# PSUM places in a fixed turn, an earlier emptying of the P V bank, and a respaced preparation table

## The chip, the cores and the metric

The kernel runs on one core of one Trainium2 chip. The metric is the device time of one execution in microseconds; the time of a kernel is the median of its runs. Five engines of the core matter here: TensorE (PE in the profile; PEld is its loading of the stationary operand), VectorE (DVE), ScalarE (ACT), GpSimd (POOL) and SyncE (SP), which issues most of the transfers.

## The reference

The computation is an attention whose queries are pooled by two, and a mixture of experts behind it that sends every row to one expert. Cut to what matters:

```python
# attention: q, k, v are (8 batches, 8 heads, 1152, 64); pooled queries: 576 per head
q_pool = q.reshape(B, H, S // 2, 2, D).mean(axis=3)
scores = (1 / sqrt(D)) * q_pool @ k^T
scores = scores - max(scores, axis=-1)
attn   = exp(scores); attn = attn / (sum(attn) + 1e-9)
x      = attn @ v                      # heads side by side: x is (4608, 512)
# experts: 8 of them, w1 (512, 1024), w2 (1024, 512)
logits = x @ w_gate
e_idx  = argmax(logits);  gate_w = softmax(logits)[e_idx]
eom    = sigmoid(x @ w_output_gate)
for e in range(8):
    m = e_idx == e
    out[m] = gate_w[m] * eom[m, e] * (relu(x[m] @ w1[e]) @ w2[e])
```

All inputs and the output are float32. The kernel splits operands into a high and a low part and adds the products, so that low-precision passes of TensorE give the accuracy of float32.

## The kernel before, in words

**Stages.** The attention takes the first two thirds of the time, the experts the rest. The attention runs over 32 pairs, a pair being two heads of one batch, four pairs to a batch. A pair takes 18 steps, one for each block of 128 keys of each head; below, "step 13" is the step with number 13 of its pair, counted from 0. The instructions of TensorE, VectorE, ScalarE and GpSimd run in the order in which the program writes them; the main loop over `s` (step) is that order.

**A step** writes, in this order: the low-part subtraction of the step before, where VectorE has it (`lo`, L289); one item of the list `fill`; the scores of the block (L279 and L281 on PE) and its exponentials on ScalarE, which go into a high part `ph` and a low part `pl` (steps 1, 3, 7, 9, 13 and 15 leave the subtraction to VectorE: L285, L286, L289; the others to GpSimd: L293, L294, L295); up to three entries of the preparation of a later pair; the row maxima of a later pair, one chunk in an even step and two in an odd one (L232 on PE into a PSUM place called `mp`, L233 on VectorE out of it, and after each chunk one item of `fill`); P V, the product of the probabilities and the values, in even steps (L308 to L310, with a delay of six steps, two or three blocks at a time, into the bank `av`); and in odd steps a piece of the router, which works on a finished pair's rows (L370 to L473).

**Emptying the bank of P V.** When a head's nine blocks are done, three items go to the front of `fill`: `e0` (the row sums scaled, into `r`, L317), `e1` (their reciprocal, L320) and `e2` (the rows times `r` into `xb`, L323). The next head's P V starts by writing out all of `fill`, and uses the same single bank, so its first product waits for `xb`.

**PSUM places.** Scores have a pool of two places (`ps_s`), P V one (`ps_a`), and everything else three (`ps_m`): the maxima's `mp`, the transposed maxima (L259), the scale's product (`gmax`, L175) and the router's pieces, which are all called `tp`. When a tile is asked for, the pool hands out one of its places, by its own account of which becomes free first; the new user waits for the last user of that place.

**Preparation.** While a pair is worked on, a later one is loaded, split and scaled. The table `PREP` says when: each entry is a number in thirds of a step and a piece of work. `kh` and `qh` are ScalarE's copies of the keys and queries (L133, L142), `kl`, `ql` and `qd` GpSimd's differences, `dk`, `dq`, `dl` transfers that place the parts (issued by SP), `lk` and `lv` loads. `amax` takes ScalarE's sum of absolute values (L171), `gmax` adds it over the partitions on PE (L175), `scale` turns the sum into a power of two in three operations (`ex` on VectorE, L180; `inv` on GpSimd, L182; `sc` on VectorE, L184), and `vh`, `vs`, `vl` split the scaled values (L187, L191, L194). From the ninth pair on, the position in the pair at which an entry is written is its number plus 51, modulo 54, in thirds of a step.

**The last pair** has no later pair to prepare and no maxima left. ScalarE and VectorE convert the first expert's weights there (`w1h`, L733, and `w1l`, L734, items of `fill`).

Of the kernel before, what the change touches and what calls it, by code (L numbers as in the profile page):

```python
# [8 lines left out]
F32 = mybir.dt.float32  # L9
# [13 lines left out]
RI = 7  # L23
PREP = ((0, 'lk'), (12, 'kh', 0), (13, 'kh', 1), (12, 'qsum'), (15, 'kl'), (18, 'dk', 0), (19, 'dk', 1), (21, 'qh'), (26, 'ql'), (26, 'dq', 0), (27, 'dq', 1), (29, 'qd'), (32, 'dl', 0), (33, 'dl', 1),
        (53, 'lv'), (71, 'amax', 0), (74, 'amax', 1), (81, 'gmax'), (82, 'scale', 0), (85, 'scale', 1), (90, 'scale', 2), (93, 'vh', 0), (93, 'vs', 0), (96, 'vh', 1), (97, 'vl', 0), (100, 'vs', 1), (104, 'vl', 1))
BURST = {0: 2, 2: 2, 4: 2, 6: 2, 8: 1, 10: 2, 12: 2, 14: 2, 16: 3}
# [33 lines left out]
def attention(tc, qT, kT, vL, wg, keep, xrows, idscr, cum, pairs, setup, scat, init):  # L60
    nc = tc.nc
    nb = len(pairs) // 4
    with ExitStack() as ctx:
# [10 lines left out]
        p3 = pool("a_p3")  # L74
        ps_s = pool("ps_s", 2, space=PSUM)
        ps_a = pool("ps_a", 1, space=PSUM)
        ps_m = pool("ps_m", 3, space=PSUM)

# [24 lines left out]
        def prep(n, table):  # L103
# [69 lines left out]
            def gmax():  # L173
                g = ps_m.tile([128, 512], F32, name="tp", tag="mp")[:, 0:2]
                nc.tensor.matmul(g, lhsT=onesf, rhs=am, start=True, stop=True)  # L175
                gm.append(g)
# [33 lines left out]
        def mgen():  # L210

            for n in range(len(pairs)):
# [3 lines left out]
                for t0, t1 in ((0, 5), (5, 9)):  # L216
# [3 lines left out]
                    for i, (t, c) in enumerate(ch):  # L220
                        mp = ps_m.tile([128, 512], F32, name=f"mp{n}", tag="mp")[:, 0:384]
                        cs = slice(384 * c, 384 * c + 384)
                        ops = []
                        mt = mtile(t)
                        for (h, o) in mt:
                            ops.append((qa[:, o:o + 128], ka[:, h, cs]))
                            if len(mt) == 1:
                                ops.append((qb[0:66, h, 128 * t if h == 0 else 64 + 128 * (t - 5):][:, 0:128], kb[0:66, h, cs]))
                        if len(mt) == 2:
                            ops.append((st['qd'], st['kp'][:, cs]))  # L230
                        for j, (l, r) in enumerate(ops):
                            nc.tensor.matmul(mp, lhsT=l, rhs=r, start=j == 0, stop=j == len(ops) - 1)  # L232
                        nc.vector.tensor_reduce(out=pm[:, i:i + 1], in_=mp, axis=AX.X, op=ALU.max)  # L233
                        pop()
                        if i < len(ch) - 1:
                            yield
# [18 lines left out]
        def rows(force=False):  # L255
            while pend_t and (force or now[0] >= pend_t[0][-1] + TLAG):
                m9, nt, t0, t1, qbf, _ = pend_t.pop(0)
                tp = ps_m.tile([128, 512], F32, name="tp", tag="mp")[0:nt, 0:128]
                nc.tensor.transpose(out=tp, in_=m9[:, 0:nt], identity=ident)  # L259
# [9 lines left out]
        def scores(st, h):  # L269
            ka, kb, qa, qb = st['ka'], st['kb'], st['qa'], st['qb']  # L270
            o = h * (NQ + 64)
            for c in range(NC):
# [3 lines left out]
                st['ph', h, c], st['pl', h, c] = ph, pl  # L276
                sps = ps_s.tile([128, 2, 512], F32, name=f"sps{st['n']}", tag="sps")
                for j in range(2):
# [19 lines left out]
        def av(st, h, xb):  # L298
# [16 lines left out]

            def e0():
                nc.vector.tensor_scalar(out=r, in0=av_[:, :, 64], scalar1=1e-9 * math.exp(SHIFT), scalar2=st['sc'][:, h:h + 1], op0=ALU.add, op1=ALU.mult)  # L317

            def e1():
                nc.vector.reciprocal(out=r, in_=r)  # L320

            def e2():
                nc.vector.tensor_tensor(out=xb[:, :, 64 * H:64 * H + 64], in0=av_[:, :, 0:64], in1=r.unsqueeze(2).broadcast_to([128, 5, 64]), op=ALU.mult)  # L323
                if h == 1:
                    routers.append([logits(st['p'][0], st['p'][1], xb), 0])
            fill[0:0] = [e0, e1, e2]
            pop(IMM)
            yield

        routers = []  # L330

        def psum():
            return ps_m.tile([128, 512], F32, name="tp", tag="mp")

# [61 lines left out]
        def router(b, xb):  # L396
# [4 lines left out]
            nc.gpsimd.iota(tid[:, 4], pattern=[[0, IW]], base=b * NQ + NQ - 128, channel_multiplier=1)  # L401
            tl = psum()

# [31 lines left out]
            so = sm.tile([128, 5, 8], F32, name="so", bufs=2)  # L435
            V.tensor_tensor(out=so, in0=og, in1=ohb, op=ALU.mult)
            yield 1
            rk = psum()
            rv = cut(rk, 0, 5, 8)
# [32 lines left out]
            V.tensor_reduce(out=cs, in_=ohb.rearrange("p t e -> p e t"), axis=AX.X, op=ALU.add)  # L472
            V.tensor_tensor(out=cum, in0=cs, in1=cum, op=ALU.add)  # L473
            for t in range(5):
                for _ in range(3):
                    yield
                i = nc.gpsimd.indirect_dma_start(
                    out=idscr, out_offset=bass.IndirectOffsetOnAxis(ap=pi[:, t:t + 1], axis=0),
                    in_=tid[:, t], in_offset=None, bounds_check=NID - 1, oob_is_err=False)
                for q in scat:  # L480
                    tc.declare_no_dep(i.ins, q, reason="distinct slots")
                scat.append(i.ins)
                if t == 2 and b < nb - 1:
                    wr()
# [40 lines left out]
        with tc.manual_schedule(engines={E.PE, E.DVE, E.Activation, E.Pool}):  # L525
# [15 lines left out]
            for s in range(18 * NP + 14):  # L541
# [14 lines left out]
                adv('m', mg, mw)  # L556
                rows()
                j = s - ALAG
                for _ in range(BURST.get(j % 18, 0) if 0 <= j < 18 * NP else 0):
# [430 lines left out]
```

## Time and profile before

| what | us |
| --- | --- |
| time, median of 3 runs | 1626.42 (1622.76 to 1629.04) |
| the profiled execution, its own time | 1624.72 |
| its span | 1622.7 |
| PE busy (share of the span) | 1533.1 (94%) |
| DVE, ACT, POOL busy | 1073.4, 1078.5, 996.3 |
| start of the first score of pair 10, step 2 | 362.61 |
| the same of the next pair's step 2 | 394.68 |

The span goes from the first to the last instruction of the trace; the rest of the profiled execution's time lies around it. In the rows of a timeline the columns are start in us, duration in us, engine, line, operation, what it writes and reads, and in brackets the idle time of the engine before it with what ended that time. Matmuls overlap each other in the pipeline, so the distance between two starts is what one costs; a matmul row with "x2" is two instructions. A pair takes 32.07 us by the last two rows of the table.

### The profile page before, as it was taken

Reading aid. Unit: us, or ns where it says so; the run is one execution under the profiler, and the core shown is the slowest. Engines: PE = TensorE matmul, PEld = TensorE weight load, DVE = VectorE, ACT = ScalarE, POOL = GpSimd, SP = SyncE. Lnnn points to the kernel's source line nnn. Section 1 sums busy time; section 2 is a strip of 40 time slices with the busy share of each in tenths; the row PEclk is TensorE's granted clock in tenths of the full one; section 3 lists DMA queues with packets and bytes.
Section 4 is the critical chain, followed back from the end, with each engine's and each line's share of the span. In section 5 each row is a group of like instructions: output and inputs, shape, how many; then the busy total and the mean of one; then the engine's idle time right before and its main releaser. Section 6 shows DMA issues by size and latency. Waiting matters only on the chain. (4 is left out here: it accounts for less than half of the span.)

```text
span 1622.7 us, 42199 instructions
## 1 busy us (share of the span) xinstructions
PE 1533.1 (94%) x16618; PEld 1411.1 (87%) x16618; DVE 1073.4 (66%) x2222; ACT 1078.5 (66%) x1862; POOL 996.3 (61%) x917
## 2 busy tenths in 40 slices
PE   4999999999999999999999999879999999999997
PEld 4898889888988888888888888868999999999996
DVE  4676776776676676676677767656666566656663
ACT  2887778877878787878777877744445444544541
POOL 4887888788879788879788978634222322232300
PEclk9999999999999999999999999979999999999999
DMA  7765455655566457446645664255454655263600
GB/s 207 217 160 143 133 149 149 156 139 141 152 151 158 124 144 189 129 123 175 158 129 153 161 154 127 83 173 196 168 190 156 213 176 194 94 226 107 208 22 25
DMA packets 88754, 245.48 MB, mean 151 GB/s; under 512 B 13082, under 2 KB 17370, under 8 KB 88546
## 3 DMA queue, kind: packets, MB, share of 16 engines
q1 hardware_dynamic: 78826, 221.07, 48.6%
q0 software_dynamic: 9728, 21.67, 4.2%
q8 instruction: 134, 2.20, 0.6%
q14 instruction: 66, 0.54, 0.1%
HBM read 165.04 MB, written 23.81 MB: 116 GB/s over the span
## 5 line engine op out<-in xcount | busy, mean ns | idle before, releaser
L233 DVE TENSOR_REDUCE pm<-mp 128x1 f32<-128x384 f32 x864 | 457.6, 549 | 263.3 <-PE mp L232 257.7
L295 POOL TENSOR_TENSOR pl<-p,ph 128x576 f16<-128x576 f32 x381 | 490.2, 1287 | 187.8 <-ACT ph L294 155.5
L232 PE MATMUL mp<-ka,qa 128*128 128x384 f32 x960 | 317.7, 347 | 20.2 <-DMA qa<-yq 18.5
L293 ACT ACTIVATE p<-sps 128x576 f32<-128x576 f32 x381 | 251.0, 659 | 116.8 <-PE sps L281 108.3
L308 PEld LDWEIGHTS <-ph 128*128 128x128 f16 x2880 | 262.6, 97 | 74.3 <-DVE xb L323 40.8
L308 PE MATMUL av<-vt,ph 128*128 128x65 f16 x2880 | 297.0, 194 | 23.4 <-DVE xb L323 23.4
L279 PE MATMUL sps<-qa,ka 128*128 128x288 f32 x1152 | 281.6, 326 | 16.7 <-ACT ph L294 10.9
L309 PE MATMUL av<-vt,ph 128*128 128x64 f16 x2880 | 294.7, 195 | 0.0
L310 PE MATMUL av<-vt,pl 128*128 128x65 f16 x2880 | 293.8, 193 | 0.0
L309 PEld LDWEIGHTS <-ph 128*128 128x128 f16 x2880 | 266.2, 97 | 0.4
L310 PEld LDWEIGHTS <-pl 128*128 128x128 f16 x2880 | 266.5, 99 | 0.0
L232 PE MATMUL mp<-kb,qb 66*128 66x384 f32 x768 | 262.5, 342 | 0.6 <-DMA kb<-kp 0.6
L281 PE MATMUL sps<-qb,kb 68*128 68x288 f32 x1152 | 248.5, 298 | 2.8 <-DMA qb<-mr 2.8
L294 ACT ACTIVATE ph<-sps 128x576 f16<-128x576 f32 x381 | 249.3, 654 | 0.0
L279 PEld LDWEIGHTS sps<-qa,ka 128*128 128x128 f32 x1152 | 183.5, 191 | 27.9 <-ACT ph L294 19.2
L764 PE MATMUL hps<-xh,w1h 128*128 128x256 f32 x704 | 200.4, 285 | 0.0
L764 PE MATMUL hps<-xl,w1h 128*128 128x256 f32 x704 | 200.3, 284 | 0.0
L232 PEld LDWEIGHTS mp<-ka,qa 128*128 128x128 f32 x960 | 180.4, 192 | 22.8 <-issue 18.5
L764 PE MATMUL hps<-xh,w1l 128*128 128x256 f32 x704 | 199.6, 284 | 0.0
L767 ACT ACTIVATE hh<-hps 128x512 fp32r<-128x512 f32 x88 | 52.7, 598 | 221.1 <-PE hps L764 221.1
L285 ACT ACTIVATE ph<-sps 128x576 f16<-128x576 f32 x195 | 128.9, 661 | 92.0 <-PE sps L281 89.7
L281 PEld LDWEIGHTS sps<-qb,kb 68*128 68x128 f32 x1152 | 186.7, 191 | 3.2 <-DMA qb<-mr 3.2
(170 smaller groups left out, 3184.6 us busy)
## 6 DMA issues: line engine op xcount, KB each, us to landing
ka<-xk SPq DMA_DIRECT2D x128, 288.0 KB
raw1b<-in_w_dram SPq DMA_DIRECT2D x24, 1024.0 KB
raw2b<-in_w_dram SPq DMA_DIRECT2D x24, 1024.0 KB
raw1a<-in_w_dram SPq DMA_DIRECT2D x22, 1024.0 KB
raw2a<-in_w_dram SPq DMA_DIRECT2D x22, 1024.0 KB
qp<-in_qT_dram SPq DMA_DIRECT2D x32, 576.0 KB
kpf<-in_kT_dram SPq DMA_DIRECT2D x32, 576.0 KB
vp<-in_vL_dram SPq DMA_DIRECT2D x32, 576.0 KB
```

The lines of the kernel that those rows point to most:

```text
L232: nc.tensor.matmul(mp, lhsT=l, rhs=r, start=j == 0, stop=j == len(ops) - 1)
L233: nc.vector.tensor_reduce(out=pm[:, i:i + 1], in_=mp, axis=AX.X, op=ALU.max)
L279: nc.tensor.matmul(sps[:, j, 0:288], lhsT=ka[:, h, ks], rhs=qa[:, o + 288 * j:o + 288 * j + 288], start=True, stop=False)
L281: nc.tensor.matmul(sps[:, j, 0:288], lhsT=kb[:, h, ks], rhs=qb[:, h, 288 * j:288 * j + 288], start=False, stop=True)
L285: nc.scalar.activation(out=ph2, in_=x, func=AF.Exp, scale=1.0 / 16)
L293: nc.scalar.activation(out=p32.rearrange("p (j n) -> p j n", j=2), in_=x, func=AF.Exp, scale=1.0 / 16)
L294: nc.scalar.activation(out=ph2, in_=x, func=AF.Exp, scale=1.0 / 16)
L295: nc.gpsimd.tensor_tensor(out=pl, in0=p32, in1=ph, op=ALU.subtract)
L308: nc.tensor.matmul(av_[:, qb, 0:65], lhsT=hi, rhs=vt[:, h, c, 0:65], start=c == 0 and qb == 0, stop=False)
L309: nc.tensor.matmul(av_[:, qb, 0:64], lhsT=hi, rhs=vt[:, h, c, 66:130], start=False, stop=False)
L310: nc.tensor.matmul(av_[:, qb, 0:65], lhsT=lo, rhs=vt[:, h, c, 0:65], start=False, stop=c == NC - 1 and qb == 4)
L764: nc.tensor.matmul(hp[:, f], lhsT=W1[w][:, c, fs], rhs=d[x][:, c], start=i == 0, stop=i == 11)
```

## The change

Three things are changed.

- The two pools of PSUM places are replaced by tiles with a name of their own for each place. Scores take place 0 or 1 by the parity of the block's number. The `mp` and `tp` tiles take three places in a fixed turn; the router's two long-lived tiles hold theirs, which the turn then leaves out, until the router has written its last use of them.
- `e0` and `e1` become one item of `fill`, so that the reciprocal stands right behind `r`, and `e2` comes one chunk of maxima earlier. When all maxima are written (in the last pair), two more items of `fill` are written in each step.
- The table `PREP` has new numbers from its third entry on. In the steady part of the loop the positions in the pair (step and third) change so: `kh 1` 5.1 to 6.2; `kl` 6.0 to 7.0; `qh` 8.0 to 8.1; `lv` 0.2 to 4.0; `amax` 6.2 and 7.2 to 10.1 and 12.1; `gmax` 10.0 to 13.1; `scale 0` 10.1 to 14.0, `scale 1` 11.1 to 14.1, `scale 2` 13.0 to 16.0; `vh 0` 14.0 to 16.1; `vh 1` 15.0 to 0.2 of the next pair.

```diff
-        (53, 'lv'), (71, 'amax', 0), (74, 'amax', 1), (81, 'gmax'), (82, 'scale', 0), ...
+        (63, 'lv'), (82, 'amax', 0), (88, 'amax', 1), (91, 'gmax'), (93, 'scale', 0), ...
...
-        ps_s = pool("ps_s", 2, space=PSUM)
+        ps_s = pool("ps_s", 1, space=PSUM)
         ps_a = pool("ps_a", 1, space=PSUM)
-        ps_m = pool("ps_m", 3, space=PSUM)
+        ps_m = pool("ps_m", 1, space=PSUM)
+        ring = [0, set()]
+
+        def psum(hold=False, name="tp"):
+
+            ring[0] = next(i % 3 for i in range(ring[0] + 1, ring[0] + 4) if i % 3 not in ring[1])
+            if hold:
+                ring[1].add(ring[0])
+            x = ps_m.tile([128, 512], F32, name=name, tag=f"mp{ring[0]}")
+            return (x, ring[0]) if hold else x
...
-                g = ps_m.tile([128, 512], F32, name="tp", tag="mp")[:, 0:2]
+                g = psum()[:, 0:2]
...
-                        mp = ps_m.tile([128, 512], F32, name=f"mp{n}", tag="mp")[:, 0:384]
+                        mp = psum(name=f"mp{n}")[:, 0:384]
...
-                tp = ps_m.tile([128, 512], F32, name="tp", tag="mp")[0:nt, 0:128]
+                tp = psum()[0:nt, 0:128]
...
-                sps = ps_s.tile([128, 2, 512], F32, name=f"sps{st['n']}", tag="sps")
+                sps = ps_s.tile([128, 2, 512], F32, name=f"sps{st['n']}", tag=f"sps{(c + 9 * h) % 2}")
...
-            def e0():
+            def e01():
                 nc.vector.tensor_scalar(out=r, in0=av_[:, :, 64], ...)
-
-            def e1():
                 nc.vector.reciprocal(out=r, in_=r)
...
-            fill[0:0] = [e0, e1, e2]
+            fill[0:0] = [e01, e2]
...
-            tl = psum()
+            tl, tk = psum(True)
...
+            ring[1].discard(tk)
             yield 1
-            rk = psum()
+            rk, rkk = psum(True)
...
             V.tensor_tensor(out=cum, in0=cs, in1=cum, op=ALU.add)
+            ring[1].discard(rkk)
...
                 rows()
+                if pos['m'] == 27 * NP:
+                    pop(2)
```

The new lines shift the later ones, so that L289 of before is L298, L233 is L242, L232 is L241, and so on. The order of the instructions moves at three places that matter below. The first is VectorE at steps 5 and 6 of a pair; before:

```order
L233 TENSOR_REDUCE pm<-mp_7285 128x1
L317 TENSOR_SCALAR r<-av_7065,sc 128x5
L233 TENSOR_REDUCE pm<-mp_7352 128x1
L320 RECIPROCAL r<-r 128x5
L233 TENSOR_REDUCE pm<-mp_7358 128x1
L323 TENSOR_TENSOR xb<-av_7065,r 128x5x64
L233 TENSOR_REDUCE pm<-mp_7377 128x1
```

and with the change:

```order
L326 TENSOR_SCALAR r<-av_7061,sc 128x5
L327 RECIPROCAL r<-r 128x5
L242 TENSOR_REDUCE pm<-mp_7353 128x1
L330 TENSOR_TENSOR xb<-av_7061,r 128x5x64
L242 TENSOR_REDUCE pm<-mp_7358 128x1
L242 TENSOR_REDUCE pm<-mp_7375 128x1
```

The reciprocal moved ahead of the first maximum of step 5, and `xb` ahead of the second. The second place is steps 13 and 14. VectorE before:

```order
L184 RECIPROCAL sc<-inv_6478 128x2
L233 TENSOR_REDUCE pm<-mp_7666 128x1
L233 TENSOR_REDUCE pm<-mp_7670 128x1
L389 TENSOR_TENSOR lT<-tp,lT 32x320
L289 TENSOR_TENSOR pl<-sps_7658,ph 128x576
L233 TENSOR_REDUCE pm<-mp_7692 128x1
```

and with the change:

```order
L242 TENSOR_REDUCE pm<-mp_7661 128x1
L242 TENSOR_REDUCE pm<-mp_7667 128x1
L393 TENSOR_TENSOR lT<-tp,lT 32x320
L298 TENSOR_TENSOR pl<-sps_7654,ph 128x576
L189 TENSOR_SCALAR ex<-tp 128x2
L242 TENSOR_REDUCE pm<-mp_7688 128x1
```

The first operation of the scale, `ex`, now stands behind the low-part subtraction of step 13 and ahead of the maximum of step 14. PE at the same place with the change (before, the same rows without L184, which stood in step 10):

```order
L241 MATMUL mp_7661<-ka_120,qa_123 128x384
L241 MATMUL mp_7661<-kb_117,qb_126 128x384
L184 MATMUL tp<-am,onesf 128x2
L241 MATMUL mp_7667<-ka_120,qa_123 128x384
L241 MATMUL mp_7667<-kb_117,qb_126 128x384
L389 MATMUL tp<-xh,wgt 128x320
L389 MATMUL tp<-xl,wgt 128x320
L288 MATMUL sps_7678<-qa_125,ka_122 128x288 x2
L290 MATMUL sps_7678<-qb_128,kb_119 128x288 x2
L241 MATMUL mp_7688<-ka_120,qa_123 128x384
L241 MATMUL mp_7688<-kb_117,qb_126 128x384
```

In the fixed turn of three, counted from the first row, `mp_7661` has the first place, the product of `gmax` (L184) the second, `mp_7667` the third, the router's `tp` (L389) the first again, and `mp_7688` the second, which `ex` reads last. The third place is VectorE in steps 4 to 8 of the last pair; before:

```order
L289 TENSOR_TENSOR pl<-sps_21727,ph 128x576
L317 TENSOR_SCALAR r<-av_21573,sc 128x5
L734 TENSOR_TENSOR w1l<-raw1a,w1h 128x1024
L289 TENSOR_TENSOR pl<-sps_21795,ph 128x576
L320 RECIPROCAL r<-r 128x5
L323 TENSOR_TENSOR xb<-av_21573,r 128x5x64
L734 TENSOR_TENSOR w1l<-raw1a,w1h 128x1024 x3
```

and with the change:

```order
L298 TENSOR_TENSOR pl<-sps_21727,ph 128x576
L326 TENSOR_SCALAR r<-av_21569,sc 128x5
L327 RECIPROCAL r<-r 128x5
L330 TENSOR_TENSOR xb<-av_21569,r 128x5x64
L298 TENSOR_TENSOR pl<-sps_21796,ph 128x576
L742 TENSOR_TENSOR w1l<-raw1a,w1h 128x1024
L298 TENSOR_TENSOR pl<-sps_21851,ph 128x576
```

All of the emptying now stands ahead of the expert weights, and the weights' subtractions come one at a time.

More of the change, by code (lines that the diff above doesn't have):

```diff
@@ L23 @@
 RI = 7
-PREP = ((0, 'lk'), (12, 'kh', 0), (13, 'kh', 1), (12, 'qsum'), (15, 'kl'), (18, 'dk', 0), (19, 'dk', 1), (21, 'qh'), (26, 'ql'), (26, 'dq', 0), (27, 'dq', 1), (29, 'qd'), (32, 'dl', 0), (33, 'dl', 1),
-        (53, 'lv'), (71, 'amax', 0), (74, 'amax', 1), (81, 'gmax'), (82, 'scale', 0), (85, 'scale', 1), (90, 'scale', 2), (93, 'vh', 0), (93, 'vs', 0), (96, 'vh', 1), (97, 'vl', 0), (100, 'vs', 1), (104, 'vl', 1))
+PREP = ((0, 'lk'), (12, 'kh', 0), (12, 'qsum'), (17, 'kh', 1), (18, 'kl'), (18, 'dk', 0), (19, 'dk', 1), (22, 'qh'), (24, 'dq', 0), (25, 'dq', 1), (26, 'ql'), (29, 'qd'), (30, 'dl', 0), (32, 'dl', 1),
+        (63, 'lv'), (82, 'amax', 0), (88, 'amax', 1), (91, 'gmax'), (93, 'scale', 0), (94, 'scale', 1), (99, 'scale', 2), (100, 'vh', 0), (101, 'vs', 0), (103, 'vl', 0), (107, 'vh', 1), (107, 'vs', 1), (110, 'vl', 1))
 BURST = {0: 2, 2: 2, 4: 2, 6: 2, 8: 1, 10: 2, 12: 2, 14: 2, 16: 3}
@@ L330, in attention @@
         routers = []
-        def psum():
-            return ps_m.tile([128, 512], F32, name="tp", tag="mp")
         wf = bp.tile([128, 4, 16], F32, name="wf")
```

## Prediction

> **What bounds the kernel now.** I read the busy times first, then the engines by stretches, then what TensorE waited for in the steady part of the attention (160 to 1040 us), then the timelines of one pair. The busy times, and the stretch 400 to 600 us (columns: length, busy time of PE, PEld, DVE, ACT, POOL with their instructions, granted PE clock, DMA share, GB/s):
>
> ```profile
> PE 1533.1 (94%) x16618; PEld 1411.1 (87%) x16618; DVE 1073.4 (66%) x2222; ACT 1078.5 (66%) x1862; POOL 996.3 (61%) x917
> 400.00:600.00 200.00, 192.35 (x2575) 177.76 (x2574) 141.11 (x357) 159.54 (x300) 159.36 (x143) 1.00 0.55 141
> ```
>
> PE is busy 192.35 of 200 us, at full clock, and no other engine comes above 160. So PE sets the time; an edit pays only by what it takes from PE's idle time, about 4% here. What the loading half of PE waited for (us in total, times, longest):
>
> ```profile
> PEld L308 <- DVE xb L323: 30.9, 47, 0.7
> PEld sps L279 <- ACT ph L294: 18.7, 52, 0.6
> PEld tp L370 <- DVE pm L233: 4.7, 8, 0.6
> ```
>
> 47 waits of P V for `xb` are about two a pair in 27 steady pairs; 52 waits of scores for ScalarE are also two a pair. Together they are 49.6 us. That is all that the change can win there.
>
> **The change part by part.** All times of steps below are from pair 10, whose stalls repeat in the other pairs. A stall is the start of a PE instruction less the time at which PE could have issued it (the start of the one before plus its usual distance).
>
> *Emptying the bank (steps 6 and 16).* VectorE, then PE, in step 6:
>
> ```profile
> 369.87 0.22 DVE L317 TENSOR_SCALAR r<-av,sc 128x5 f32<-128x5 f32 x1 [0.39 <-PE av L310]
> 370.83 0.56 DVE L233 TENSOR_REDUCE pm<-mp 128x1 f32<-128x384 f32 x1 [0.74 <-PE mp L232]
> 371.31 0.18 DVE L320 RECIPROCAL r<-r 128x5 f32<-128x5 f32 x1
> 371.40 0.52 DVE L233 TENSOR_REDUCE pm<-mp 128x1 f32<-128x384 f32 x1
> 371.84 0.48 DVE L323 TENSOR_TENSOR xb<-av,r 128x320 f32<-128x320 f32 x1
> ...
> 371.69 0.33 PE L232 MATMUL mp<-kb,qb 66*128 66x384 f32 x1
> 372.37 0.20 PE L308 MATMUL av<-vt,ph 128*128 128x65 f16 x1 [0.35 <-DVE xb L323]
> ```
>
> PE could have started at 371.69 + 0.18 = 371.87 and started at 372.37: 0.50 lost. With the change the reciprocal falls into the 0.74 of idle time ahead of 370.83, and `xb` follows the first maximum at 371.31 and ends at 371.79, before 371.87. The stall goes; the margin is only 0.08, less the 0.05 that PE took after `xb`. The second maximum comes 0.4 later, and nothing on PE asks for its place at once. Step 16 has the same pattern.
>
> *Places of the scores (steps 3 and 15).*
>
> ```profile
> 365.37 0.64 ACT L294 ACTIVATE ph<-sps 128x576 f16<-128x576 f32 x1
> 365.22 0.73 DVE L289 TENSOR_TENSOR pl<-sps,ph 128x576 f16<-128x576 f32 x1
> 365.82 0.19 PE L310 MATMUL av<-vt,pl 128*128 128x65 f16 x1
> 366.07 0.53 PE L279 MATMUL sps<-qa,ka 128*128 128x288 f32 x2
> ```
>
> The scores of step 3 wait for ScalarE's second exponential of step 2 (365.37 + 0.64 = 366.01): the pool gave them the place of step 2, not that of step 1. PE could have gone on at 365.85. In the fixed order they take the place of step 1, which VectorE leaves at 365.22 + 0.73 = 365.95. So of the 0.22 stall some 0.08 goes and 0.14 stays. In step 15 the place of step 13 is long free.
>
> *The scale's product and the places behind it (steps 10, 13, 14).* This is the new cost. PE, then VectorE, then the two short operations that move (their groups):
>
> ```profile
> 385.47 0.34 PE L232 MATMUL mp<-kb,qb 66*128 66x384 f32 x1
> 385.65 0.31 PE L385 MATMUL tp<-xh,wgt 128*128 128x320 f32 x1
> 386.47 0.34 PE L232 MATMUL mp<-ka,qa 128*128 128x384 f32 x1
> 387.91 0.53 PE L279 MATMUL sps<-qa,ka 128*128 128x288 f32 x2 [0.46 <-ACT ph L294]
> 389.95 0.33 PE L232 MATMUL mp<-kb,qb 66*128 66x384 f32 x1
> 390.63 0.20 PE L308 MATMUL av<-vt,ph 128*128 128x65 f16 x1 [0.35 <-DVE xb L323]
> 391.56 0.51 PE L279 MATMUL sps<-qa,ka 128*128 128x288 f32 x2
> ...
> 385.49 1.02 DVE L233 TENSOR_REDUCE pm<-mp 128x1 f32<-128x384 f32 x2 [0.67 <-PE mp L232]
> 386.43 0.47 DVE L389 TENSOR_TENSOR lT<-tp,lT 32x320 f32<-32x320 f32 x1
> 386.83 0.73 DVE L289 TENSOR_TENSOR pl<-sps,ph 128x576 f16<-128x576 f32 x1
> 389.09 0.56 DVE L233 TENSOR_REDUCE pm<-mp 128x1 f32<-128x384 f32 x1 [0.93 <-PE mp L232]
> L180 DVE TENSOR_SCALAR ex<-tp x32: 139/150/151, 30.5 to 1030.9; 128x2 uint32<-128x2 uint32 x32
> L175 PE MATMUL tp<-am,onesf x64: 165/246/251, 29.6 to 1029.4; 128*128 128x2 f32 x64
> ```
>
> `gmax` leaves step 10 (there it takes about 0.14 of PE and a stall of 0.08, both estimates from starts) and comes between the two maxima of step 13. Now follow the turn of three. The router's `tp` gets the place of the first maximum, so it waits until VectorE has read that: 385.49 + 0.56 = 386.05, PE at 386.10, where it could have come at 385.65 + 0.14 = 385.79: a stall of 0.3. VectorE then does `lT` (386.58 to 387.05) and `lo` (386.98 to 387.72), and only then `ex`, 0.15 long, until 387.78. The maximum of step 14 has `gmax`'s place and waits for `ex`: PE comes to it at 386.47 + 0.14 + 0.3 = 386.9, and starts at 387.83. A stall of 0.9. Behind the waiting matmul stand the P V of step 14 and the scores of step 15, which ScalarE waits for. From 387.83 the maximum costs 0.35 and one block of P V 0.47, so step 15 starts at 388.66 instead of 387.91: +0.75. Its own stall for ScalarE is gone. The P V of step 16, relieved of `xb`, comes at 390.13 + 0.75 = 390.88 instead of 390.63, and step 17 loses 0.16 to `lo` of step 15, whose place it now has: 391.97 instead of 391.56, +0.41.
>
> A plain pair therefore changes by -0.08 (step 3) - 0.50 (step 6) - 0.22 (step 10) + 0.41 = -0.39. There are 13 of these. In the 7 pairs that open a batch step 16 had no wait, and 0.16 at step 17 is there before, so with less to win they come to -0.05.
>
> *The router (7 pairs, the second of a batch), step 7.*
>
> ```profile
> 342.47 0.44 PE L370 MATMUL tp<-ident,xb 128*128 128x128 f32 x2 [0.30 <-DVE pm L233]
> 341.86 1.02 DVE L233 TENSOR_REDUCE pm<-mp 128x1 f32<-128x384 f32 x2 [0.80 <-PE mp L232]
> 343.06 0.17 DVE L473 TENSOR_TENSOR cum<-tp,cum 128x8 bf16<-128x8 f32 x1
> ```
>
> These transposes take the place that the allocator gave, free behind the first of two maxima. In the turn they take the router's just released place, whose last user is `cum`: 343.23 instead of 342.42, so PE starts 0.8 later. These pairs come to -0.39 + 0.8 = +0.4.
>
> Sum of the steady pairs: 13 x -0.39 + 7 x -0.05 + 7 x 0.4 = -2.6.
>
> *ScalarE.* `amax` moves into steps 10 and 12. Ahead of step 13's exponentials:
>
> ```profile
> 385.14 0.65 ACT L285 ACTIVATE ph<-sps 128x576 f16<-128x576 f32 x1 [0.79 <-PE sps L281]
> ...
> 373.82 0.70 ACT L171 ACTIVATE junk<-vp 128x576 f16<-128x576 f32 x1
> 374.49 0.67 ACT L285 ACTIVATE ph<-sps 128x576 f16<-128x576 f32 x1
> ```
>
> 0.79 is idle; `amax` with its read-out costs about 0.67 (in step 7 it held the next instruction back from 373.82 to 374.49). It fits, with 0.1 to spare. If it did not, `lo`, `ex` and PE would be late by the rest. The copies `kh` and `qh` move by a third or a step at most; their transfers keep steps of lead. The first four pairs win about 2 (one loses 2.8 to `gmax` and a slower clock before; an estimate of what its new wait leaves).
>
> *The last pair.*
>
> ```profile
> 1054.61 2.94 ACT L733 CAST w1h<-raw1a 128x1024 fp32r<-128x1024 f32 x3
> 1055.15 0.23 PE L308 MATMUL av<-vt,ph 128*128 128x65 f16 x1 [3.53 <-DVE xb L323]
> 1075.97 0.65 ACT L285 ACTIVATE ph<-sps 128x576 f16<-128x576 f32 x1 [3.31 <-PE sps L281]
> ```
>
> PE idles 3.53 there because `xb` stands behind a weight subtraction; that wait goes, and a like one at step 16. ScalarE with its exponentials and casts then binds; I put its last exponentials at about 1071.7, 4.3 earlier (an estimate from its row of work, with the casts one in two steps). Both ends: 0, if the casts spread over the steps delay ScalarE by as much, and 6, the two waits.
>
> **The sum.** -2.6 - 2 - 4.3 = -8.9 on the profiled execution's 1624.72, 1615.8. That execution lies 1.7 under the median, so on the median's scale 1617.5; I say 1617. The bounds: the new waits at step 14 cost nothing if `ex` gets through earlier (27 x 0.75 = 20 less), or 0.5 a pair more if ScalarE is late (13.5 more).
>
> **The rivals.**
>
> *The waits go and none comes.* `ex` would have to pass VectorE before PE asks for the place. For it: `gmax` itself ends at 385.5, well ahead. Against it: the written order has `lo` in front. Then the 49.6 of the waits' table, less 4 for step 3, go, with the last pair's: about 1626 - 46 - 6 = 1574; if half comes through, 1600.
>
> *ScalarE becomes the place where it is lost.* The margin of 0.1 at step 13 is thinner than the spread of these estimates. If `amax` pushes the exponentials by 0.4 to 0.5, `lo`, `ex` and PE at step 14 follow: 27 x 0.45 = 12 more, 1629. It decides from a push of 0.3 (27 x 0.3 = 8, all of the gain).
>
> *The clock drops (slower).* Two neighbouring windows of 3.41 us before:
>
> ```profile
> 148.30:151.71 3.41, 1.86 (x21) 1.61 (x20) 1.98 (x6) 2.63 (x7) 3.14 (x3) 1.00 1.02 241
> 151.71:155.12 3.41, 3.41 (x35) 3.22 (x32) 0.90 (x4) 0.94 (x2) 1.00 (x3) 0.50 0.88 192
> ```
>
> PE was busy 1.86 of 3.41, and the next 3.41 us ran at half clock. With the change the stalls of 0.3 and 0.9 lie within 2.2 us of each other, and that window would hold some 3.41 - 1.2 = 2.2 to 2.5 of busy time; at step 7 of the router's pairs likewise. If the point is near there, some 16 windows at half clock follow, each worth 1.7: +27, less 9: 1644. Against it: 2.2 is above 1.86, and no steady pair of before shows a drop. [...]
>
> *It does not do what it says.* The places could come out as before; against it, the names are fixed. Then 1626.
>
> **How the numbers follow.** A measurement of this kernel tells about 0.5%, 8 us, from no change: faster is below 1618, slower above 1635. My forecast 0.52, and as it lies at the edge, 0.3 of that faster and 0.22 same. No new wait, or half of it: 0.15, faster. ScalarE: 0.20, of it 0.16 same, 0.02 on either side. The clock: 0.09, slower. Nothing changes: 0.04, of it 0.03 same. Faster 0.48, same 0.41, slower 0.11. The range runs from 1600 to 1633; it leaves out the full gain below and the clock above, some 2 in 10.
>
> **What would show it.** Right: `xb` gone from PE's waits at steps 6 and 16; a wait of PE for `ex` (now L189) at step 14 in nearly every steady pair, 0.6 to 0.9 long; PE waiting for `cum` in 7 pairs; the last pair without the 3.53. Wrong: no wait for `ex`; `amax` with step 13's exponentials right behind it and no idle time; a granted clock of 0.5 in the steady part; or the copies and differences of the preparation late, so that PE waits for a transfer into `ka`, `qa` or `qb`.

## The result and the profile after

The changed kernel takes 1639.5 us (median of 6 runs, 1635.92 to 1645.68), the kernel before 1625.26 beside it: a ratio of 1.0089, 95% interval 1.0073 to 1.0106. Timed again later it took 1639.8, at a ratio of 1.0077 (1.0049 to 1.0104). It is slower by some 14 us, 0.8 to 0.9%; 1617 was forecast, with a range from 1600 to 1633. The first profile after is of the slowest of its six executions (1645.68); a second, of an execution of 1640.49, lies nearer the median, and both are used below.

Two things in the part ahead of the prediction need setting right. The position of a table entry in a steady pair is its number plus 3, modulo 54 (not plus 51), and this holds from the sixth pair on (not the ninth); the positions listed there are right. And the two starts that its table gives for step 2 (362.61 and 394.68) are those of step 1, by the count of steps that the rest of the text uses; their distance, 32.07, is a pair all the same.

The shares of the engines are as before, and so is the steady stretch from 400 to 600 us (same columns as before):

```profile
PE 1541.7 (94%) x16618; PEld 1414.5 (86%) x16618; DVE 1087.1 (66%) x2222; ACT 1089.1 (66%) x1862; POOL 991.9 (60%) x917
400.00:600.00 200.00, 192.36 (x2540) 177.19 (x2538) 141.40 (x345) 162.24 (x299) 158.48 (x145) 1.00 0.58 147
```

PE issued 2540 matmuls in these 200 us, 2575 before: as busy, a little less done, at full clock. What the loading half of PE waited for from 160 to 1040 us:

```profile
PEld mp L241 <- DVE ex L189: 27.3, 27, 1.2
PEld tp L389 <- DVE pm L242: 10.2, 26, 0.4
PEld tp L374 <- DVE cum L478: 9.9, 7, 1.4
PEld L317 <- DVE xb L330: 8.9, 46, 1.8
```

The 30.9 us for `xb` fell to 8.9 (of the matmuls themselves only one still waits for it, in pair 26), and the 18.7 for ScalarE's exponentials are gone from this list; 27 waits for `ex`, 26 of the router's product for the first maximum and 7 for `cum` came in their place. Pair 10, steps 13 to 15, selected rows of PE with one row of its loading half, and then VectorE:

```profile
395.63 0.34 PE L241 MATMUL mp<-kb,qb 66*128 66x384 f32 x1
396.04 0.42 PE L389 MATMUL tp<-xh,wgt 128*128 128x320 f32 x1
396.15 0.19 PEld L389 LDWEIGHTS tp<-xl,wgt 128*128 128x128 f32 x1
396.30 0.31 PE L389 MATMUL tp<-xl,wgt 128*128 128x320 f32 x1
396.71 0.43 PE L290 MATMUL sps<-qb,kb 68*128 68x288 f32 x2
397.91 0.44 PE L241 MATMUL mp<-ka,qa 128*128 128x384 f32 x1 [0.77 <-DVE ex L189]
398.19 0.33 PE L241 MATMUL mp<-kb,qb 66*128 66x384 f32 x1
...
395.43 1.14 DVE L242 TENSOR_REDUCE pm<-mp 128x1 f32<-128x384 f32 x2 [0.92 <-PE mp L241]
396.65 0.48 DVE L393 TENSOR_TENSOR lT<-tp,lT 32x320 f32<-32x320 f32 x1
397.05 0.73 DVE L298 TENSOR_TENSOR pl<-sps,ph 128x576 f16<-128x576 f32 x1
397.72 0.14 DVE L189 TENSOR_SCALAR ex<-tp 128x2 uint32<-128x2 uint32 x1
```

This is the chain that the prediction wrote down: the first maximum, the router's product, `lT`, `lo`, `ex`, and only then the maximum of step 14. The loss is not there alone, as a table by parts shows. The time from the start of one part to the next, from the first score rows of each step:

| part (us) | before | changed | changed, second profile |
| --- | --- | --- | --- |
| to step 0 of pair 2 | 99.2 | 110.8 | 106.8 |
| pairs 2 and 3 | 66.0 | 63.7 | 63.7 |
| pairs 4 to 25 | 714.9 | 720.8 | 720.3 |
| pair 26 | 32.9 | 39.8 | 39.8 |
| pairs 27 to 30 | 129.9 | 130.7 | 132.1 |
| from pair 31 to the end | 579.8 | 578.2 | 576.1 |
| span | 1622.7 | 1644.0 | 1638.8 |

Three places lose: the start, the steady pairs, and pair 26 by itself.

**The start.** SP's transfers ahead of pair 1, before and changed:

```profile
61.20 0.59 SPq L101 DMA_DIRECT2D kb<-kp  x1
61.89 1.61 SPq L101 DMA_DIRECT2D qb<-mr  x2
63.55 0.53 SPq L101 DMA_DIRECT2D qa<-yq  x1
```

```profile
64.08 0.58 SPq L110 DMA_DIRECT2D kb<-kp  x1
65.05 0.46 SPq L110 DMA_DIRECT2D qa<-yq  x1
66.24 0.46 SPq L110 DMA_DIRECT2D kb<-kp  x1
67.05 2.01 SPq L110 DMA_DIRECT2D qb<-mr  x2
...
63.76 0.28 DVE L272 SCALAR_TENSOR_TENSOR mr<-tp,mr 5x128 fp32r<-5x128 f32 x1
```

The two transfers of the row maxima (`mr` into `qb`) stood behind two of `dl`'s four; now they stand behind all four. VectorE has written `mr` at 64.04, SP issues it at 67.05. PE's first scores of the pair need `qb`. PE's row in the changed kernel; two stretches of 5 us of it, and behind the dots the second of them in the kernel before; and the sum of this wait up to 110 us, before and then changed:

```profile
73.15 0.82 PE L290 MATMUL sps<-qb,kb 68*128 68x288 f32 x2 [3.19 <-DMA qb<-mr]
```

```profile
70.00:75.00 5.00, 1.85 (x15) 1.58 (x16) 0.76 (x2) 1.22 (x3) 1.27 (x1) 0.76 0.86 252
75.00:80.00 5.00, 5.00 (x38) 4.76 (x35) 2.12 (x6) 2.50 (x5) 3.25 (x3) 0.50 0.00 0
...
75.00:80.00 5.00, 5.00 (x92) 4.66 (x91) 4.14 (x11) 3.74 (x7) 3.21 (x4) 1.00 0.67 216
```

```profile
PE sps L281 <- DMA qb<-mr: 2.8, 2, 2.2
```

```profile
PE sps L290 <- DMA qb<-mr: 8.4, 2, 5.2
```

The waits are 5.6 us longer, and from 75 to 80 us, behind the wait of 3.19, the granted clock is 0.50, where it was 1.00 before. Over the two stretches around these waits, 33 to 52 and 67 to 86 us, it is 0.64 and 0.73 in the changed kernel, 0.82 and 1.00 before. I put the rest of the 11.6 us, 6.0, down to the clock, an estimate by subtraction; no run takes the two apart.

**Pair 26.** In this pair VectorE does short operations for the setup of the experts. Two long ones with a short one between them, and GpSimd at the same time:

```profile
903.78 2.99 DVE L645 COPY cb<-cum 128x8 bf16<-128x8 bf16 x1
912.87 0.15 DVE L655 TENSOR_REDUCE mx<-cn 128x1 f32<-128x8 f32 x1
913.05 4.01 DVE L656 TENSOR_TENSOR cn<-cn,mx 128x8 f32<-128x8 f32 x1
...
904.19 2.55 POOL L304 TENSOR_TENSOR pl<-p,ph 128x576 f16<-128x576 f32 x2
906.90 0.99 POOL L483 DMA_INDIRECT idscr<-tid,posi  x1 [0.17 <-DMA qb<-mr]
911.78 2.66 POOL L145 TENSOR_TENSOR kp<-kpf,xk 128x1152 fp32r<-128x1152 f32 x1
914.41 1.28 POOL L304 TENSOR_TENSOR pl<-p,ph 128x576 f16<-128x576 f32 x1
915.65 1.39 POOL L154 TENSOR_TENSOR yq<-yq,xq 128x576 fp32r<-128x576 f32 x1
917.01 1.27 POOL L304 TENSOR_TENSOR pl<-p,ph 128x576 f16<-128x576 f32 x1
```

Before, the same copy fell on a pause of GpSimd, and the same comparison took 0.28:

```profile
888.73 0.16 DVE L637 COPY cb<-cum 128x8 bf16<-128x8 bf16 x1
888.75 1.29 POOL L295 TENSOR_TENSOR pl<-p,ph 128x576 f16<-128x576 f32 x1 [0.16 <-ACT ph L294]
...
897.75 0.28 DVE L648 TENSOR_TENSOR cn<-cn,mx 128x8 f32<-128x8 f32 x1
```

Eight columns of a copy take 2.99 us instead of 0.16. It ends at 906.77, 0.03 after GpSimd's row of subtractions (906.74); the comparison ends at 917.06, 0.02 after the third of GpSimd's operations that it met (917.04), though a fourth follows without a pause. Both read and write SBUF alone: a copy, and an operation with two inputs. The maxima and subtractions of the steady pairs read PSUM and keep their 0.55 and 0.75; the maximum at 912.87, with SBUF alone but one input, took 0.15 in the middle of a GpSimd operation. Behind each long one stands VectorE's `xb` or a maximum, and PE waits for those, 1.5 and 1.9; from 920 to 925 us, behind the second, the granted clock is 0.50. In the four profiles here where neither the copy nor a two-input operation of this setup took over 2 us, pair 26 takes 32.1 to 32.9; in the ten others, 34.8 to 39.8.

### The profile page after: what moved, and what is told of

The parts are those of the page before. It is cut to its first block, busy times and chain, and to the rows that moved or that the text cites. A ratio compares the mean times of both kernels' runs of the same rounds, so it can differ in the third digit from the quotient of the medians.

```text
span 1644.0 us, 42280 instructions
## 1 busy us (share of the span) xinstructions
PE 1541.7 (94%) x16618; PEld 1414.5 (86%) x16618; DVE 1087.1 (66%) x2222; ACT 1089.1 (66%) x1862; POOL 991.9 (60%) x917
## 5 line engine op out<-in xcount | busy, mean ns | idle before, releaser
L242 DVE TENSOR_REDUCE pm<-mp 128x1 f32<-128x384 f32 x864 | 460.6, 552 | 289.6 <-PE mp L241 284.4
L241 PE MATMUL mp<-ka,qa 128*128 128x384 f32 x960 | 321.0, 351 | 43.3 <-DVE ex L189 22.6
L241 PE MATMUL mp<-kb,qb 66*128 66x384 f32 x768 | 263.7, 343 | 0.6 <-DMA kb<-kp 0.6
L241 PEld LDWEIGHTS mp<-ka,qa 128*128 128x128 f32 x960 | 180.9, 192 | 52.5 <-DVE ex L189 29.8
L290 PEld LDWEIGHTS sps<-qb,kb 68*128 68x128 f32 x1152 | 188.6, 192 | 10.1 <-DMA qb<-mr 10.1
```

The costliest lines, as they stand in the source:

```text
L290: nc.tensor.matmul(sps[:, j, 0:288], lhsT=kb[:, h, ks], rhs=qb[:, h, 288 * j:288 * j + 288], start=False, stop=True)
```

## The experiments

All are compared with the kernel before in the same runs. "Step 6 to 7" means the distance of the first score rows of these steps, median over the plain pairs (the third and fourth of a batch, without pair 26).

**`dl` back in the table.**

```diff
-(30, 'dl', 0), (32, 'dl', 1)
+(32, 'dl', 0), (33, 'dl', 1)
```

> The changed kernel with one edit: the table's `dl` entries back to 32 and 33 (they were 30 and 32). Theory A: at the start the changed kernel writes more of `dl`'s four transfers into SP's queue ahead of the two that carry the row maxima (`mr` into `qb`), the first scores of pairs 0 and 1 wait 2.6 to 3 us longer, and PE's clock halves behind the wait; the edit puts SP's order back, takes some 10 to 11 us off and comes to about 1629, with step 0 of pair 2 near 100 us instead of 110.8. Rival B: the loss is in the steady pairs (waits on places); then the edit takes off under 3, 1637 to 1640.

Measured: 1633.63, ratio 1.0064 (1.0042 to 1.0086). SP issues `mr` behind two transfers again, at 63.76; the wait up to 110 us is 3.4 instead of 8.4, and pair 2 begins at 100.91. That is the mechanism of theory A. Its size in time is smaller than the 10 to 11 us expected: 6 us by the medians of runs that were not made side by side, and the intervals of the two ratios overlap. Over all kernels here, pair 2 begins at 104.3 to 110.8 us with `dl` at 30 and 32 (four profiles) and at 97.8 to 103.0 with 32 and 33 (ten, before among them). The rest of the loss, in the steady pairs and in pair 26, stays: there B holds.

**The table as before, the rest changed** (PREP replaced by that of before).

> The changed kernel with the whole of PREP as before; the fixed turn of places and the earlier emptying stay. Theory A and C (C: in the steady pairs the table's `gmax` in step 13 makes PE wait for `ex` in step 14 and for the first maximum in step 13, 1.4 a pair, and that eats what steps 6, 15 and 16 give back): start as before, steps 6, 15 and 16 free, about 1.2 a pair less than before in 27 pairs, the router's 0.8 in 7 pairs stays: 1625 - 32 + 6 - 3 = about 1596. Rival D: it is the fixed turn itself that costs, whatever the table; then new waits of PE for a place stand in other steps and the time is 1615 to 1630.

Measured: 1612.63, 0.9938 (0.9915 to 0.9961). Faster, but by 11 and not 29. Steps 6 and 16 are free, steps 13 and 14 have no wait, and the start is at 98.9. But step 7 to 9 grew from 3.51 to 3.91: what step 6 gave came back at step 9. Step 15 still waits for `lo` of step 13 (step 14 to 15 takes 1.77, and 1.49 with `ex` early, below), and the router's 0.8 stayed. Neither theory had the give-back at step 9; since the next kernel has it without the fixed turn, it is not the turn's.

**The earlier emptying alone.**

```diff
-            fill[0:0] = [e0, e1, e2]
+            fill[0:0] = [e01, e2]
+                if pos['m'] == 27 * NP:
+                    pop(2)
```

> The kernel before with the second part alone: reciprocal behind `r`, `xb` ahead of the second maximum, two more items of `fill` in a step of the last pair. Theory: the waits for `xb`, 0.5 in step 6 of 27 pairs and in step 16 of 20, go and nothing takes their place: 23 less, and 2 to 4 in the last pair, about 1599. Rival E: what steps 6 and 16 give is lost again in steps 15 and 17 (scores that wait for ScalarE, which is at its own pace): half, about 1612, or nothing.

Measured: 1608.75, 0.9914 (0.9894 to 0.9934): 15 us, between the two. Step 6 to 7 falls from 2.31 to 1.80, step 16 to 17 from 2.32 to 2.08, step 7 to 9 rises from 3.51 to 3.91. ScalarE is the reason, with the copies and `amax` of the old table in steps 5 to 8 (its read-outs, 0.22 each, left out):

```profile
370.38 0.70 ACT L171 ACTIVATE junk<-vp 128x576 f16<-128x576 f32 x1
371.05 0.67 ACT L285 ACTIVATE ph<-sps 128x576 f16<-128x576 f32 x1
371.58 0.68 ACT L286 ACTIVATE sps<-sps 128x576 f32<-128x576 f32 x1
372.15 0.70 ACT L171 ACTIVATE junk<-vp 128x576 f16<-128x576 f32 x1
372.81 0.39 ACT L372 CAST xh<-tp 128x256 fp32r<-128x256 f32 x1
...
373.27 0.50 PE L279 MATMUL sps<-qa,ka 128*128 128x288 f32 x2 [0.23 <-DVE pl L289]
```

It has no pause here, so PE, earlier by 0.5, waits for what ScalarE and the subtraction behind it release. With the new table step 9 has no such wait (3.51 in the changed kernel): this is what the spacing of ScalarE's work is worth.

**The scores' places alone.**

```diff
-tag="sps")
+tag=f"sps{(c + 9 * h) % 2}")
```

> The kernel before with the scores' two places by the block's parity, and no other edit. Theory: the wait of step 15's scores for ScalarE, 0.62 to 0.73 in 27 pairs, goes; step 17 gets 0.16 to 0.26 for VectorE's subtraction; step 3 stays, since its new place is left at nearly the same time: 12 to 14 less, about 1612. Rival F: the pool's choice was the better one, the wait moves on to step 16 (`xb`) or 17 whole: 1623 to 1627.

Measured: 1619.69, 0.9983 (0.9971 to 0.9994): 3 to 4 us, a quarter of what was expected. Step 14 to 15 falls from 1.97 to 1.77, by 0.20 where 0.62 to 0.73 was expected: the place of step 13 is not long free; VectorE's `lo` leaves it, and PE's list has now 25 waits for that:

```profile
PE sps L279 <- DVE pl L289: 7.6, 25, 0.5
```

Step 3 gains nothing: step 2 to 3 takes 2.15 instead of 2.11, step 3 to 4 1.30 instead of 1.35. The rival, that the wait moves to 16 or 17, does not hold.

**`ex` one third of a step earlier.**

```diff
-(93, 'scale', 0)
+(92, 'scale', 0)
```

> The changed kernel with one number: `scale 0` at 92 instead of 93, so that `ex` stands on VectorE right behind the two maxima of step 13 and ahead of `lT` and `lo`. Theory C: PE's wait of 1.0 in step 14 is for the place that `ex` empties last; it goes. Step 15's scores then come early enough to wait for `lo` of step 13, whose place they take in the fixed turn (0.5, as the kernel with the scores' places alone shows), so 0.5 a pair is left over, 27 times: 13 less than the changed kernel, about 1625. Rival: step 14 waits for VectorE's `lT` or for the maxima anyway; then nothing changes, 1638.

Measured: 1611.17, 0.9919 (0.9891 to 0.9947): 28 us less than the changed kernel, by one number in the table. The 27 waits for `ex` are down to one, and PE gets more into the steady stretch:

```profile
400.00:600.00 200.00, 195.64 (x2608) 180.91 (x2605) 144.27 (x364) 164.92 (x306) 164.42 (x147) 1.00 0.57 145
```

```profile
PEld mp L241 <- DVE ex L189: 0.8, 1, 0.8
```

Step 14 to 15 falls from 2.39 to 1.49, and step 15 gives back 0.13, not the 0.5 that was expected, since step 13's wait stays and gives `lo` its time. So theory C holds in kind, at twice the size expected. Of the 28 us, 22 to 23 lie in pairs 4 to 30 without pair 26; the rest lies in the start and in pair 26, which also differ between kernels that share this table. The wait at step 14 thus cost more than the whole of what the change lost.

**`gmax` in step 14, `dl` back, the router's place held longer.**

```diff
-(91, 'gmax'), (93, 'scale', 0), (94, 'scale', 1), (99, 'scale', 2), (100, 'vh', 0), ...
+(94, 'gmax'), (96, 'scale', 0), (97, 'scale', 1), (102, 'scale', 2), (103, 'vh', 0), ...
-            ring[1].discard(rkk)
             for t in range(5):
                 for _ in range(3):
                     yield
+                    ring[1].discard(rkk)
```

> The changed kernel with `dl` at 32 and 33, `gmax` in step 14 behind its only maximum (94), `scale` at 96, 97 and 102 and the split of the values behind it (103 to 112), and the router's second place held one piece longer, so that the transposes of step 7 don't get it. Theory C: steps 13 and 14 lose their 0.45 and 0.96, step 15 gets 0.4 for `lo`, step 7 of the router's pairs loses 0.8: 27 x 1.0 + 7 x 0.8 = 33 less than with `dl` alone (1633.6), about 1601. Rival: the later split of the values collides with ScalarE's exponentials of steps 17 and 0, and half of it is lost, 1615.

Measured: 1592.91, 0.9798 (0.9772 to 0.9824), faster than both kernels. A plain pair takes 30.86 us:

| plain pair (us) | before | changed | `ex` early | `gmax` in 14 |
| --- | --- | --- | --- | --- |
| step 6 to 7 | 2.31 | 1.80 | 1.80 | 1.80 |
| step 10 to 11 | 2.12 | 1.89 | 1.89 | 1.89 |
| step 13 to 14 | 1.61 | 2.17 | 2.17 | 1.61 |
| step 14 to 15 | 1.97 | 2.39 | 1.49 | 1.77 |
| step 16 to 17 | 2.32 | 2.08 | 2.08 | 2.08 |
| the pair | 32.07 | 32.04 | 31.14 | 30.86 |
| the first pair of a batch | 32.33 | 32.49 | 31.57 | 31.28 |
| the second | 33.37 | 34.03 | 33.09 | 32.05 |

Three edits were made at once here, so the time does not tell them apart; the plain pair's steps 13 to 15 show the first, the second pair of a batch the last. Pair 26 still takes 38.3.

**All but the fixed turn** (the emptying alone, with the new table and `dl` at 32 and 33).

> The kernel before with the earlier emptying and the new table with `dl` at 32 and 33: all but the fixed turn of places. Theory: the pool gives step 14's maximum the place of step 13's second maximum instead of `gmax`'s, so the wait for `ex` is not there; the router's transposes keep their place; step 13's wait for the first maximum stays, 15 keeps its 0.7: 27 x (1.0 - 0.6) + 7 x 0.8 = 16 less than the kernel that differs by the turn (1633.6), about 1617. Rival: `gmax` in step 13 makes PE wait under any choice of places; then 1628 to 1634.

Measured: 1603.58, 0.986 (0.9833 to 0.9888). The pool gives step 14's maximum another place than `gmax`'s, as the theory has it, and step 13's wait stays. The kernel with `dl` at 32 and 33 (1633.63, ratio 1.0064) differs from this one by the fixed places alone, the scores' two and the turn of three: with this table they cost about 30 us against the pool.

**The table alone** (PREP replaced in the kernel before).

> The kernel before with the new table alone. Theory A: the start loses what the changed kernel lost, step 0 of pair 2 comes near 105 to 111 us instead of 99.2; the steady pairs keep 0.5 in steps 6 and 16 and get 0.45 in step 13: about 1623.7 + 8 + 27 x 0.3 = 1640. Rival: the start's loss needs the fixed turn or the earlier emptying; then pair 2 begins at 99 to 101 us and the time is 1626 to 1632.

Measured: 1625.75, 1.0008 (0.9994 to 1.0021), no clear change. The start is lost, as in theory A: pair 2 begins at 106.8, and the wait is there:

```profile
PE sps L281 <- DMA qb<-mr: 9.7, 2, 6.2
```

The rest was too dark a forecast: step 10 gains, and what step 13 loses step 15 gives back, so a plain pair takes 31.88, less than before.

**The setup's operations off SBUF.**

```diff
-        V.tensor_copy(out=cb, in_=self.cum)
+        nc.scalar.copy(out=cb, in_=self.cum)
-        V.tensor_tensor(out=cn, in0=cn, in1=mx..., op=ALU.is_equal)
+        V.tensor_tensor(out=cn, in0=cp[:, 0:8], in1=mx..., op=ALU.is_equal)
```

> The kernel with `gmax` in step 14 (1592.9), and in the setup of the experts, which falls into pair 26, two VectorE operations that read and write SBUF alone are put elsewhere: the copy `cb` on ScalarE, and the comparison reads the counts where they stand in PSUM. Theory H: those two took 2.8 and 4.2 us instead of 0.2 and 0.3 because each went on until GpSimd's row of work behind another had its next gap (its end is within 0.05 us of the end of a GpSimd operation), and PE waited behind them for 4 to 6 us; pair 26 falls from 38.3 to 32 to 33 us, and the time by 5 to 6, to about 1587. Rival: the two are slow from something else in that pair (transfers into the same memory), and the operations behind them become slow in their place; then 1592.

Measured: 1593.75, 0.9804 (0.9783 to 0.9824): no gain. The two operations took 0.20 and 0.17, but the next one that reads SBUF alone, a product, took the wait over:

```profile
870.73 4.47 DVE L660 TENSOR_TENSOR cn<-cn,em 128x8 f32<-128x8 f32 x1
873.88 1.29 POOL L305 TENSOR_TENSOR pl<-p,ph 128x576 f16<-128x576 f32 x1
```

Its end, 875.20, is again 0.03 behind the end of a GpSimd operation, 875.17. The rival's time came, so this run alone does not settle theory H; in the last experiment, with the product off SBUF as well, pair 26 takes 32.8.

**`lo` ahead of `mr` and `lT`.**

```diff
                 adv('m', mg, mw)
+                if s % 18 in (1, 13):
+                    while pendv:
+                        pendv.pop(0)()
                 rows()
```

> The last one and one more edit: in steps 1 and 13 VectorE's `lo` of the step is written right behind the step's maxima, ahead of the row maxima's `mr` and of the router's `lT`, instead of at the start of the next step. Theory: the scores of steps 3 and 15 wait only for the place that `lo` empties (0.33 and 0.37, of which 0.08 and 0.05 are no wait), so 0.25 and 0.3 a pair go: 27 x 0.55 = 15 less, about 1573. Rival: the rows of the maxima come 0.7 later and the first scores of a pair wait for them, or `lT` comes late and PE waits for its place in step 15; then less than 5.

Measured: 1589.82, 0.9765 (0.9737 to 0.9793). Steps 3 and 15 lose their waits (step 2 to 3 falls from 2.16 to 1.90, step 14 to 15 from 1.77 to 1.47) and a plain pair can take 30.3 us, but the first scores, most of all in the last pair of a batch, now wait 6.9 us in all for the row maxima (six waits, up to 1.6; 1.7 in three without this edit). Behind three of these, of 1.4 to 1.6 us, the granted clock is 0.50 for 3.4 us (from 382.4, 508.7 and 635.0). In the main, it is the rival.

**The changed kernel once more.**

> The changed kernel once more, with a second profile, to see which of its losses are there in every execution. Theory A: the start's loss (step 0 of pair 2 at 110.8 instead of 99.2 us) is there again, 5 to 12 us; theory H: pair 26 is again some 4 us or more above the 33 of before; time about 1638. Rival: the first profile was an odd one, and the start is at 99 to 101 us.

Measured: 1639.8. The table above has its parts: the start and pair 26 lose again, the start 4 us less than in the first profile.

**Both repairs together**: `lo` early in step 13 alone, and the comparison writes its result into PSUM, where the product reads it.

```diff
+                if s % 18 == 13:
-        V.tensor_tensor(out=cn, in0=cn, in1=em, op=ALU.mult)
+        V.tensor_tensor(out=cn, in0=cp[:, 8:16], in1=em, op=ALU.mult)
```

> The kernel with `gmax` in step 14, `lo` written early in step 13 alone (in step 1 it held the row maxima's transfers back), and all three short operations of the experts' setup moved off SBUF alone: `cb` on ScalarE, the comparison and the product read PSUM. Theory H: no operation of that setup is then longer than 0.5 us, and pair 26 takes 31 to 33 us instead of 37.6 to 38.3. Theory for `lo`: step 15 loses its 0.3 in 27 pairs and nothing is late for it: 8 less. Together 1592.9 - 5 - 8 = about 1580. Rival: a further operation of the setup takes the wait over, pair 26 stays at 37, 1585.

Measured: 1581.87, 0.9743 (0.9727 to 0.9759), the fastest here. The three operations are short and pair 26 takes 32.8, as theory H has it:

```profile
864.37 0.15 DVE L655 COPY cn<-tp 128x8 f32<-128x8 f32 x1
866.26 0.17 DVE L660 TENSOR_TENSOR tp<-tp,mx 128x8 f32<-128x8 f32 x1
868.66 0.15 DVE L662 TENSOR_TENSOR cn<-tp,em 128x8 f32<-128x8 f32 x1
```

One later operation of the setup, with two inputs in SBUF (`oh`, at 871.21), took 1.78, above the 0.5 of the theory, and again ended 0.03 behind a GpSimd operation; PE waits 0.27 for a maximum behind it. Step 14 to 15 falls to 1.47 as with `lo` early in both steps, but the first scores of the last pair of a batch wait 4.9 us in all for the row maxima (five waits; 2.5 in four with `gmax` in step 14), so a part of the 8 expected of `lo` is lost again.

## Why the prediction was wrong

The forecast was a sum of three terms, 8.9 us less. Two of them came out with the other sign, and a loss stood in none: the steady pairs lost 6.7 and 7.6 us in the two profiles where a gain of 2.6 was forecast, the first four pairs lost 9.2 and 5.2 where a gain of 2 was forecast, and pair 26 lost 6.9. Every sign that the prediction named for being right was there; they cover the steady and the last pairs. Of its signs for being wrong one came as well, at the start: PE waits longer for a transfer into `qb`.

- **The emptying (steps 6 and 16): right.** Step 6 to 7 fell by 0.51 for 0.50 forecast. It came through because the new table moved `amax` away; with the old one 0.4 would have come back at step 9, which the prediction did not see.
- **Step 10: right**, 0.23 for 0.22. **Step 3: no gain**, where 0.08 was forecast: its scores come 0.04 later and the step behind them is 0.05 shorter.
- **Steps 13 to 17: the mechanism right, the size wrong.** Step 13 to 15 grew by 0.98 (0.75 forecast) and step 17 came 0.73 later (0.41 forecast). A plain pair gained 0.03 instead of 0.39, the first of a batch lost 0.16, the second 0.66 instead of 0.4: pairs 4 to 30 without pair 26 lost 6.7 and 7.6 in the two profiles, where a gain of 2.6 was forecast for all of them. The missing term is what a wait costs beyond itself: behind one, the next matmul comes 0.26 and 0.28 later instead of 0.15 and 0.18, in the rows at 396.04 and 397.91, and its weights load 0.11 and 0.10 later than the first matmul starts (396.15 and 398.01; before, the same loads began with the first matmul, at 385.65 and 386.47). That makes 0.21 of the missing 0.23. The prediction counted the wait alone. Step 17's stall for `lo`, forecast at 0.16, came to 0.26 (its scores start 0.29 behind the matmul ahead of them, 0.03 before); that is the rest.
- **"The copies move by a third or a step at most; their transfers keep steps of lead", and the first four pairs "win about 2": the step whose mechanism failed.** It holds for the steady pairs. In the start the two halves of `dl` move past the transfers of the row maxima in SP's queue, and PE is already waiting for those: the wait grew from 2.8 to 8.4 us, and the first four pairs lost 9.2 and 5.2 in the two profiles. The table alone shows this too, and `dl` at 32 and 33 takes the wait back to 3.4.
- **Pair 26 is in no part of the prediction.** It lost 6.9 us in both profiles, from the instants at which VectorE's short operations meet GpSimd. No part of the change aims at these instants; where they fall is luck.
- **The last pair: right in kind.** The wait of 3.53 is gone, and the part from pair 31 on gained 1.6 and 3.6 for 4.3 forecast.
- **The rivals.** ScalarE was not late at step 13. The clock rival's 1644 lies near the measured time by luck: the clock did not fall in the steady pairs (1.00 from 400 to 600 us, with a wait of 0.4 and one of 1.0 of the loading half in nearly every pair). It did fall behind the waits of 5.2 and 3.2 us at the start (0.50 from 40 to 45 and from 75 to 80 us), behind the 1.9 of pair 26 (0.50 from 920 to 925; behind the 1.5 ahead of it, 1.00 up to 915), and behind three of 1.4 to 1.6 in the kernel with `lo` early (0.50 for 3.4 us).

## What to carry to other kernels

When a table of work is moved, follow every entry through the filling of the pipeline as well as its steady part, and past every queue: two transfers ahead of the two that the pair's first scores need cost 5 to 9 us, about as much as all the steady pairs did. In a fixed turn of places, the one whose reader stands last in its engine's order sets the wait of the place's next user; moving that reader by one slot (`ex`, 92 for 93) was worth 0.9 us a plain pair, and moving its writer to a step with slack 1.2. An emptied wait is worth its length only if the engine that releases the next place has slack there: with the old table step 6 to 7 gave 0.51 and step 7 to 9 took 0.40 back.

## What the runs showed of the hardware that was not expected

In pair 26 a copy and two-input operations of VectorE on 128 x 8 elements in SBUF alone were long where they met a row of GpSimd operations without a pause: the copy took 2.99 us in the changed kernel and 2.97 with `dl` back, the comparison 4.01 in both, the product 4.47 with the other two off SBUF. In the kernel before the same three took 0.16, 0.28 and 0.17. Each of the long ones ended within 0.05 us of the end of a GpSimd operation, the second to the fourth that it met and not the first; yet the comparison of the kernel before got through behind the first, and that of the changed kernel behind the third, with the next GpSimd operation following at once in both. What decides how many go ahead is not shown. The two-input operations with an operand in PSUM took 0.15 to 0.17 at the same place, and the reciprocal of the emptying, with one input from SBUF, kept its 0.19 (all 64 of the changed kernel took that). The wait went on past the end of the GpSimd operation that it began in: the changed kernel's comparison began in one that ended at 914.44, and ended at 917.06.
